# Where a decode kernel's late products, first gate and residual sum stand in its tail

## The chip, the core and the metric

The kernel runs on one core of a Trainium2 chip. Its engines are named as in the profile: PE is TensorE (matmuls; PEld are its weight loads), DVE is VectorE, ACT is ScalarE, POOL is GpSimd, and SP is SyncE, which here only issues transfers. The metric is the device time of one execution in microseconds. Everything is computed in fp32.

## The reference

One token of a transformer block at decode. The block has a modulation by a vector `c`, an attention over a cache of 8192 positions with 32 heads of 192, and a feed-forward part:

```python
mod = (_silu(c) @ w_mod).reshape(c.shape[0], 6, 1, -1)
sa, ca, ga, sb, cb, gb = (mod[:, 0], mod[:, 1], mod[:, 2], mod[:, 3], mod[:, 4], mod[:, 5])
h = _layernorm(x, axis=-1) * (1 + ca) + sa
x = x + ga * _A_ref(h, A_k_cache, A_v_cache, A_wq, A_wo)
h = _layernorm(x, axis=-1) * (1 + cb) + sb
x = x + gb * _B_ref(h, B_w1, B_b1, B_w2, B_b2)
```

`_A_ref` projects to queries with wq (640 x 6144), takes the softmax of the scores against the cached keys, sums the cached values, and projects back with wo (6144 x 640). `_B_ref` is w1 (640 x 1536), a squared ReLU, and w2 (1536 x 640). The six parts of `mod` have 640 numbers each; ga, sb, cb and gb are needed only after the attention.

## The kernel before

**The main loop.** The two caches of 32 heads are 201 MB each, and nearly all of the time goes into reading them once. A head's keys lie as 64 positions in each of 128 partitions. DVE multiplies them with the query and sums over the head's 192 (L282 to L291, `dve_keys`), POOL folds a small part, ACT takes the exponential (L306), and TensorE multiplies the probabilities with the values (L226, `pe_values`) in three column groups at once. Heads go in pairs, 16 of them. Keys lie in `k_t[0]` and `k_t[1]` by turns, values in `v_t[0]` and `v_t[1]`; SP refills a buffer when its last reader is done, all on one queue.

**After a pair.** `dve_project` (L318 to L333) takes the pair's sums of values out of PSUM: a reciprocal of the sums of the exponentials, then for each of the two heads a scaled and masked copy `om` (L327) and a sum `os` (L329). TensorE turns `os` into columns (`pe_turn`, `ps_oT`), DVE copies them to `oT`. `attend` (L308 to L316) is the output projection: DVE multiplies a pair's piece of wo with its three columns and adds to `acc`, three SCALAR_TENSOR_TENSOR of 128 x 640 (L315). For most pairs this happens in the loop, with the piece of wo behind the keys in `k_t[1]`.

**The tail.** The pieces of wo of pairs 11 to 14 come together in one transfer, `wot` in `v_t[0]`, and their products are the late ones: `attend_late`. `between` calls it for pairs 11, 12 and 13 (nine products), out of `dve_project` of the last pair, after the wait for the second head's values. Pair 14 follows after the copy of the last `oT`. The piece of the last pair is done by TensorE (L427) from `wm1` in `k_t[0]`, added in PSUM (`ps_att`) to the sum of `acc` over the partitions (L419).

The other tail transfers, in the order of SP's queue, are: `wot`; `wm1` (last piece of wo and the weights of ga, sb and cb); `w1g` in two pieces (w1, then the weights of gb) into `k_t[1]`; and w2 in four pieces (6, 3, 2 and 1 blocks of 12) into `v_t[1]`, which are issued when the last values are multiplied.

**Gates and the layernorm.** `mod(target, w, n, blocks)` (L154 to L160) multiplies silu(c) with the weights of n parts of 640, block by block of 32 rows, in four column groups of n x 160. In before, one call makes ga, sb and cb together (`ps_b`, 480 columns, five blocks). DVE copies them into `mods` and adds one to cb. The residual `x1` is `ps_att` times ga (L431) plus x (L432). `layernorm` (L167 to L183) sums x1 (L170), has TensorE total it over the partitions (L164), subtracts the mean, squares and sums (L176), totals again, and has ACT take the root (L178); a reciprocal (L181) and two DVE steps with cb and sb end it. Its argument `before` is a function called between the first total and DVE's wait for it, and `scale1` one called after ACT's root is issued; in before both do nothing in the tail.

**Feed-forward.** TensorE multiplies with w1 (L441), then makes gb (L159, 160 columns). DVE adds the bias, takes the maximum with zero, squares and transposes (L448 to L451); TensorE multiplies with w2 block by block (L466) and waits for each of the four pieces ahead of its blocks. DVE multiplies with gb and adds (L469, L470), and SP stores 640 numbers.

Each engine's instructions run in the order of the program text; a semaphore wait holds all that stands behind it on that engine.

Of the kernel before, what the change touches and what calls it, by code (L numbers as in the profile page):

```python
# [5 lines left out]
ALU = mybir.AluOpType  # L6
AX = mybir.AxisListType
# [3 lines left out]
D = 640  # L11
# [5 lines left out]
DG = D // G  # L17
FG = FF // G
KB = DG // 32
# [5 lines left out]
NPAIR = H // 2  # L25
# [4 lines left out]
WO = 3 * D  # L30
# [40 lines left out]
def block_kernel(nc, kw, ky, vc, wm0, wot, wm1, w1g, w2, out):  # L71
    sem = nc.alloc_semaphore
    V, A, L, T, S = (Line(nc, e, n) for e, n in ((nc.vector, "dve"), (nc.scalar, "act"), (nc.gpsimd, "pool"),
                                                 (nc.tensor, "pe"), (nc.sync, "sp")))
    v, act, pool, pe = nc.vector, nc.scalar, nc.gpsimd, nc.tensor
# [11 lines left out]
    def ps(name):  # L87
        return nc.alloc_psum_tensor(name, [P, 512], F32)
# [15 lines left out]
    ps_mx = [ps(f"ps_mx{s}") for s in range(2)]  # L104
    ps_sum, ps_oT, ps_q, ps_att = ps("ps_sum"), ps("ps_oT"), ps("ps_q"), ps("ps_att")
    ps_o = [ps(f"ps_o{s}") for s in range(2)]
# [47 lines left out]
    def mod(target, w, n, blocks):  # L154

        for b in blocks:
            wb = w[:, b * n * D:(b + 1) * n * D].rearrange("p (m n) -> p m n", m=n)
            for g in range(G):
                i = pe.matmul(target[32 * g:32 * (g + 1), :n * DG], e_t[:, b:b + 1].to_broadcast([P, 32]),  # L159
                              wb[:, :, DG * g:DG * (g + 1)], start=(b == 0), stop=(b == KB - 1))  # L160
        return T.mark(i)

    def total(col, src):
        i = pe.matmul(ps_sum[:, col:col + src.shape[1]], ones[:, :], src, start=True, stop=True)  # L164
        return T.mark(i)

    def layernorm(x, copies, s, m, xm, sq, ss, sd, rs, h, scale1, shift, col, ready, before):  # L167

        V.wait(ready)
        T.wait(V.mark(v.tensor_reduce(s, x, axis=AX.X, op=ALU.add)))  # L170
        m_t = total(col, s)
        before()
        V.wait(m_t)
        V.wait(V.mark(v.tensor_scalar(m, ps_sum[:, col:col + 1], 1.0 / (copies * D), None, op0=ALU.mult)))
        V.wait(V.mark(v.tensor_scalar(xm, x, m, None, op0=ALU.subtract)))
        T.wait(V.mark(v.scalar_tensor_tensor(sq, xm, 1.0, xm, op0=ALU.mult, op1=ALU.mult, accum_out=ss)))  # L176
        A.wait(total(col + 1, ss))
        m_sd = A.mark(act.activation(sd, ps_sum[:, col + 1:col + 2], AF.Sqrt, bias=eps_t[:, :], scale=1.0 / (copies * D)))  # L178
        sc1 = scale1()
        V.wait(m_sd)  # L180
        V.wait(V.mark(v.reciprocal(rs, sd)))  # L181
        V.wait(V.mark(v.scalar_tensor_tensor(h, xm, rs, sc1, op0=ALU.mult, op1=ALU.mult)))  # L182
        return V.mark(v.tensor_add(h, h, shift))  # L183
# [15 lines left out]
    s_, m_, ss_, sd_, rs_ = (piece(at + j, 1) for j in range(5))  # L199
    xm_, sq_ = piece(at + 5, KB), piece(at + 5 + KB, KB)  # L200
    m_h1 = layernorm(x_c, 1, s_, m_, xm_, sq_, ss_, sd_, rs_, h1[:, :], scale_a, maT[:, :KB, 0], 8, m_small, lambda: None)

    T.wait(m_h1)
    wq0 = v_t[1][:, KB * 2 * D:KB * 2 * D + WQ].rearrange("p (b n) -> p b n", b=KB)
    for b in range(KB):
        i = pe.matmul(ps_q[:, :PW], h1[:, b:b + 1].to_broadcast([P, P]), wq0[:, b], start=(b == 0), stop=(b == KB - 1))
# [4 lines left out]
    done = {}  # L211
# [97 lines left out]
    def attend(i, w, landed):  # L309

        w = w.rearrange("p (j n) -> p j n", j=NV)
        V.wait(landed)
        for j in range(NV):
            V.wait(V.last())
            V.mark(v.scalar_tensor_tensor(acc[:, :], w[:, j], oT[:, i, j:j + 1], acc[:, :], op0=ALU.mult, op1=ALU.add))  # L315
        done["wo", i] = V.last()  # L316

    def dve_project(i, between=lambda: None):  # L318

        V.wait(done["sum", i])  # L320
        V.wait(V.mark(v.reciprocal(r2[:, :], ps_sum[:, :2])))
        for a in range(2):
            n = 32 * NV
            V.wait(done["v", 2 * i + a])
            if a:
                between()
            V.wait(V.mark(v.scalar_tensor_tensor(om[:n], ps_o[a][:n].rearrange("p (d e) -> p d e", e=E), r2[:n, a:a + 1],  # L327
                                                 mask[:n, None, :].to_broadcast([n, ED, E]), op0=ALU.mult, op1=ALU.mult)))
            o = v.tensor_reduce(os_[:n, a], om[:n], axis=AX.X, op=ALU.add)  # L329
            if a == 0:  # L330
                V.wait(V.mark(o))
        o.then_inc(tk_o, 1)
# [5 lines left out]
    for h in range(H):  # L338
        s, i = h % 2, h // 2
        def between(c):  # L340
            if s == 0 and i and c == 0:
                dve_project(i - 1)
            if s and i and c == 0 and h in WITH_W:
                attend(i - 1, k_t[1][:, HD:], (k_sem[1][1], 16 * (i + 1)))

        dve_keys(h, between)
        if s == 0 and i:
            turned(i - 1)
        if s == 0 and i + 1 < NPAIR:
            evict_query(i + 1, done["q", i + 1])  # L350
        dve_max(h)
        if h + 1 < H:
            S.wait(*(m_wm0 if h == 0 else (done["v", h - 1],)))
            dma(v_t[1 - s][:, :], vc[h + 1], b_sem[1 - s])
        if h + 2 < H:
            S.wait(*done["k", h])
            if s == 0:
                S.wait(done["q", i + 1])
            elif h in WITH_W:
                S.wait(done["wo", i - 1])  # L360
            w = KSLOT if h + 2 in WITH_W else HD
            dma(k_t[s][:, :w], keys_of(h + 2), k_sem[s][1])


    wot_t, wm1_t, w1_t, w2_t = v_t[0], k_t[0], k_t[1], v_t[1]
# [9 lines left out]
    a = 0  # L375
    for n, b in enumerate(W2_CUT):
        dma(w2_t[:, a:b], w2[:, a:b], w_sem[3 + n])
        a = b
# [3 lines left out]
    def room(n):  # L382
        r = tail[0][:, :n]
        tail[0] = tail[0][:, n:]
        return r

    mods = room(4 * DG)
    x1, x_t, gb2, y, hT, cb1, xm2, sq2, h2 = (room(DG) for _ in range(9))
    f, fT = room(FG), room(FG)
    bbt, spr = room(32 * (FB + KB)), room(32 * (FB + KB))  # L390
    s2, m2, ss2, sd2, rs2 = (room(1) for _ in range(5))

    def spread(dst, src, n):
        s3 = spr[:, :32 * n]
        V.wait(V.mark(v.tensor_copy(s3.rearrange("p (b r) -> p b r", r=32), src[:, :, None].to_broadcast([P, n, 32]))))
        V.wait(V.mark(v.transpose(dst, s3)))

    def attend_late(i):
        at = (i - NPAIR + 1 + NTAIL) * WO
        attend(i, wot_t[:, at:at + WO], (w_sem[8], 16))  # L400
# [2 lines left out]
        for i in range(NPAIR - 1 - NTAIL, NPAIR - 2):  # L403
            attend_late(i)

    ps_b, ps_g, ps_f, ps_y = ps_mx[0], ps_mx[1], ps_o[0], ps_o[1]
    dve_project(NPAIR - 1, between)
    T.take(tk_o)
    m_turn = T.mark(pe.matmul(ps_oT[:, :NV], os_[:96].rearrange("p a d -> p (a d)"), quad[:96, :], start=True, stop=True))  # L409
    T.wait((w_sem[1], 16))  # L410
    m_b = mod(ps_b, wm1_t[:, WO:], 3, range(KB))
    V.wait(m_turn)
    m_oT = V.mark(v.tensor_copy(oT[:, NPAIR - 1], ps_oT[:, :NV]))
    attend_late(NPAIR - 2)
    V.wait(done["v", H - 2])
    spread(x_t, x_c, KB)
    T.wait(done["wo", NPAIR - 2])
    for g in range(G):
        pe.matmul(ps_att[32 * g:32 * (g + 1), :DG], ones[:, :32], acc[:, DG * g:DG * (g + 1)], start=True, stop=False)  # L419
    V.wait(m_b)  # L420
    v.tensor_copy(mods[:, :3 * DG], ps_b[:, :3 * DG])
    cb1_of = V.mark(v.tensor_scalar(cb1, ps_b[:, 2 * DG:3 * DG], 1.0, None, op0=ALU.add))
    wo = wm1_t[:, :WO].rearrange("p (j n) -> p j n", j=NV)
    T.wait(m_oT)
    for j in range(NV):
        for g in range(G):
            i = pe.matmul(ps_att[32 * g:32 * (g + 1), :DG], oT[:, NPAIR - 1, j:j + 1].to_broadcast([P, 32]),  # L427
                          wo[:, j, DG * g:DG * (g + 1)], start=False, stop=(j == NV - 1))
    m_att = T.mark(i)
    V.wait(m_att, cb1_of)  # L430
    V.wait(V.mark(v.tensor_mul(x1, ps_att[:, :DG], mods[:, :DG])))  # L431
    m_x1 = V.mark(v.tensor_add(x1, x1, x_t))  # L432
    m_h2 = layernorm(x1, 32, s2, m2, xm2, sq2, ss2, sd2, rs2, h2, lambda: cb1, mods[:, DG:2 * DG], 16, m_x1, lambda: None)
    V.wait(m_h2)
    m_hT = V.mark(v.transpose(hT, h2))  # L435
    T.wait(m_hT, (w_sem[2], 16))
    hT3 = hT.rearrange("p (b r) -> p b r", r=32)
    for b in range(KB):
        at = b * FF
        for g in range(G):  # L440
            i = pe.matmul(ps_f[32 * g:32 * (g + 1), :FG], hT3[:, b], w1_t[:, at + FG * g:at + FG * (g + 1)],  # L441
                          start=(b == 0), stop=(b == KB - 1))
# [16 lines left out]
    for b in range(FB):  # L459
# [4 lines left out]
        for g in range(G):  # L464
            o = b * D + DG * g
            i = pe.matmul(ps_y[32 * g:32 * (g + 1), :DG], fT3[:, b], w2_t[:, o:o + DG], start=(b == 0), stop=(b == FB - 1))  # L466
# [50 lines left out]
```

## Time and profile before

| | before |
|---|---|
| median of 3 runs | 1063.14 us (1063.02 to 1063.73) |
| the profiled execution, its own time | 1062.42 us |
| its span, first to last instruction | 1061.1 us |
| HBM read | 451.82 MB, 426 GB/s over the span |
| DVE busy | 867.6 us (82%) |
| PE busy | 441.3 us (42%) |
| POOL busy | 195.1 us (18%) |
| ACT busy | 32.9 us (3%) |
| mean granted clock of TensorE | 0.688 |

The profile is one execution. A busy share says how much of the span an engine worked, not whether the end waited for it. The timeline gives each instruction's start and length in us from the span's start; in brackets stands how long its engine was idle before it and what ended that. A fp32 matmul stands as two rows of the trace, so 20 matmuls count as x40. The chain that ended last is followed back from the last instruction. A transfer's time runs from its issue to its landing, and so includes its wait behind the earlier ones of the queue.

### The profile page before, as it was taken

To read this page: it belongs to the slowest core of one execution; us is meant where nothing else is said; L and a number is where in the kernel's file an instruction comes from. 1 tells how busy PE (TensorE), PEld (TensorE's weight loads), DVE (VectorE), ACT (ScalarE), POOL (GpSimd) and SP (SyncE) were. 2 spreads that over 40 slices of the span, in tenths; PEclk is the share of its full clock that TensorE was granted. 3 is DMA by queue.
4 is the path that set the end of the run, shared out by engine and by line. 5 is a ranking of instruction groups with operands and counts; after the bars stand their busy time and mean duration, and the time that the engine had idled before them with its cause. 6 is when DMAs were issued, how large, how long until landed. Compare 5 with 4: busy or idle time off the path is not lost. (4 is left out here: it accounts for less than half of the span.)

```text
span 1061.1 us, 5222 instructions
## 1 busy us (share of the span) xinstructions
PE 441.3 (42%) x2130; PEld 161.5 (15%) x2130; DVE 867.6 (82%) x445; ACT 32.9 (3%) x87; POOL 195.1 (18%) x71
## 2 busy tenths in 40 slices
PE   3135423254452336345243633425354434335337
PEld 1012111021120102112011211201111111112113
DVE  1885888988888988888898888899889797998964
ACT  1000000000000000000000000000000000000000
POOL 0221212212212221221221221222122122221210
PEclk9586657686665767666676665667666666767668
DMA  9999999999999999999999999999999999999994
GB/s 396 443 441 418 438 424 447 423 443 439 413 448 426 430 435 441 434 423 434 441 421 439 443 424 438 422 441 424 443 431 431 436 426 439 428 437 434 425 424 194
DMA packets 10675, 451.95 MB, mean 426 GB/s; under 512 B 1188, under 2 KB 1192, under 8 KB 1576
## 3 DMA queue, kind: packets, MB, share of 16 engines
q1 hardware_dynamic: 10664, 451.83, 98.7%
q8 instruction: 4, 0.07, 0.0%
q14 instruction: 7, 0.06, 0.0%
HBM read 451.82 MB, written 0.00 MB: 426 GB/s over the span
## 5 line engine op out<-in xcount | busy, mean ns | idle before, releaser
L282 DVE TENSOR_TENSOR k<-k,qb 128x6144 f32<-128x6144 f32 x64 | 419.4, 6553 | 112.5 <-DMA k<-in_kw 98.9
L285 POOL TENSOR_TENSOR k<-k 128x1344 f32<-128x1344 f32 x64 | 193.9, 3029 | 815.5 <-DVE k L282 815.5
L226 PE MATMUL ps_o<-v,p 128*32 128x512 f32 x1536 | 290.7, 732 | 20.0 <-PEq L60 20.0
L287 DVE TENSOR_REDUCE sc<-k 128x18 f32<-128x3456 f32 x64 | 240.2, 3753 | 2.2
L232 PE MATMUL ps_mx<-ident,mp 128*128 128x128 f32 x64 | 24.2, 480 | 456.6 <-PEq L60 456.6
L238 PE MATMUL ps_q<-k,h 128*128 128x384 f32 x160 | 86.7, 713 | 89.6 <-PEq L60 89.6
L226 PEld LDWEIGHTS ps_o<-v,p 128*32 128x32 f32 x1536 | 73.3, 131 | 213.2 <-issue 213.0
L291 DVE TENSOR_REDUCE sc<-k 128x14 f32<-128x1344 f32 x64 | 98.7, 1543 | 0.0
L232 PEld LDWEIGHTS ps_mx<-ident,mp 128*128 128x128 f32 x64 | 15.9, 308 | 471.7 <-issue 471.5
L238 PEld LDWEIGHTS ps_q<-k,h 128*128 128x128 f32 x160 | 44.1, 286 | 135.9 <-issue 131.2
L306 ACT ACTIVATE p<-sc,nm 128x256 f32<-128x256 f32 x32 | 16.2, 508 | 654.5 <-DVE nm L300 629.2
L300 DVE TENSOR_REDUCE nm<-ps_mx 128x1 f32<-128x128 f32 x32 | 9.3, 292 | 32.2 <-PE ps_mx L232 32.2
L315 DVE SCALAR_TENSOR_TENSOR acc<-k,oT,acc 128x640 f32<-128x640 f32 x33 | 29.2, 885 | 1.2
L327 DVE SCALAR_TENSOR_TENSOR om<-ps_o,r,mask 96x512 f32<-96x512 f32 x32 | 23.9, 747 | 1.1
L329 DVE TENSOR_REDUCE os<-om 96x64 f32<-96x512 f32 x32 | 21.8, 682 | 1.1
L215 ACT ACTIVATE qb<-ps_q 128x384 f32<-128x384 f32 x16 | 7.8, 490 | 311.1 <-PE ps_q L238 304.7
L315 DVE SCALAR_TENSOR_TENSOR acc<-v,oT,acc 128x640 f32<-128x640 f32 x12 | 10.6, 885 | 7.6 <-PE ps_o L226 7.2
L247 PE MATMUL ps_sum<-sp,ones 128*128 128x2 f32 x32 | 8.9, 349 | 18.7 <-PEq L60 18.7
L159 PE MATMUL ps_o<-v,silu 128*32 128x320 f32 x40 | 5.6, 741 | 14.4 <-DVE silu L152 14.4
L247 PEld LDWEIGHTS ps_sum<-sp,ones 128*128 128x128 f32 x32 | 8.0, 312 | 23.0 <-issue 23.0
L144 DVE COPY small<-v 128x27 f32<-128x27 f32 x1 | 0.2, 180 | 11.6 <-DMA v<-in_wm 11.6
L159 PE MATMUL ps_mx<-k,silu 128*32 128x480 f32 (+1 forms) x80 | 8.2, 568 | 0.0
(74 smaller groups left out, 80.4 us busy)
## 6 DMA issues: line engine op xcount, KB each, us to landing
v<-in_vc SPq DMA_DIRECT2D x32, 6144.0 KB, 39.0
k<-in_kw SPq DMA_DIRECT2D x25, 7104.0 KB, 36.1
k<-in_ky SPq DMA_DIRECT2D x6, 6144.0 KB, 35.7
k<-in_wm SPq DMA_DIRECT2D x1, 5760.0 KB, 28.5
v<-in_wm SPq DMA_DIRECT2D x1, 4173.5 KB, 12.6
k<-in_kw SPq DMA_DIRECT2D x1, 4032.0 KB, 28.5
v<-in_wot SPq DMA_DIRECT2D x1, 3840.0 KB, 15.3
k<-in_w1g SPq DMA_DIRECT2D x1, 3840.0 KB, 23.8
```

Source lines behind the costliest of these rows:

```text
L226: i = pe.matmul(ps_o[s][32 * g:32 * (g + 1), :], p_t[s][:, E * j:E * (j + 1)].rearrange("p e r -> p (e r)"), t[:, j, g], start=(j == 0), s ...
L232: return pe.matmul(ps_mx[s][:, :P], mp[s][:, :].to_broadcast([P, P]), ident[:, :], start=True, stop=True)
L238: i = pe.matmul(ps_q[:, :PW], h1[:, b:b + 1].to_broadcast([P, P]), w[:, b], start=(b == 0), stop=(b == KB - 1))
L247: return pe.matmul(ps_sum[:, :2], ones[:, :], sp[:, :], start=True, stop=True)
L282: m_mul = V.mark(v.tensor_mul(pr, pr, q[:, None, :].to_broadcast([P, HALF, DH])))
L285: m_fold = L.mark(pool.tensor_add(half, half, pr[:, KEEP:, DH // 2:]))
L287: o = v.tensor_reduce(r[:, :KEEP], pr[:, :KEEP], axis=AX.X, op=ALU.add)
L291: m_sc = V.mark(v.tensor_reduce(r[:, KEEP:], half, axis=AX.X, op=ALU.add))
L306: act.activation(p_t[s][:, :, :], sc[s][:, :, None].to_broadcast([P, NPOS, 32 // E]), AF.Exp, bias=nm[s][:, :], accum_out=sp[:, s:s + 1]). ...
L315: V.mark(v.scalar_tensor_tensor(acc[:, :], w[:, j], oT[:, i, j:j + 1], acc[:, :], op0=ALU.mult, op1=ALU.add))
L327: V.wait(V.mark(v.scalar_tensor_tensor(om[:n], ps_o[a][:n].rearrange("p (d e) -> p d e", e=E), r2[:n, a:a + 1], mask[:n, None, :].to_broad ...
L329: o = v.tensor_reduce(os_[:n, a], om[:n], axis=AX.X, op=ALU.add)
```

## The change

1. In `dve_project` the wait for a head's values moves behind the call of `between`. In the last pair, DVE's nine late products thus stand ahead of the wait for the last head's values. For the other pairs `between` is empty there.
2. `wm1` is laid out with ga's weights apart from those of sb and cb, with the same number of bytes. `mod` makes ga alone in five blocks (into `ps_a`, the bank `ps_q`), then two blocks of sb and cb (`ps_b`). Two further blocks come in `before`, between the two totals of the layernorm, and the last one in `scale_b`, behind the second total.
3. Pair 14's products stand ahead of DVE's wait for the last turn and the copy of `oT`. DVE copies ga alone ahead of the residual; sb's copy and cb plus one follow in `scale_b`, behind the second total and ahead of the reciprocal.
4. x1's addition becomes a SCALAR_TENSOR_TENSOR which also writes the sum to `s2`; `layernorm` with `summed=True` leaves out its own sum, and TensorE waits for x1.

```diff
-    def layernorm(x, copies, s, m, xm, sq, ss, sd, rs, h, scale1, shift, col, ready, before):
-
-        V.wait(ready)
-        T.wait(V.mark(v.tensor_reduce(s, x, axis=AX.X, op=ALU.add)))
+    def layernorm(x, copies, s, m, xm, sq, ss, sd, rs, h, scale1, shift, col, ready, before, summed=False):
+
+        if summed:
+            T.wait(ready)
+        else:
+            V.wait(ready)
+            T.wait(V.mark(v.tensor_reduce(s, x, axis=AX.X, op=ALU.add)))
         m_t = total(col, s)
         before()
...
         for a in range(2):
             n = 32 * NV
-            V.wait(done["v", 2 * i + a])
             if a:
                 between()
+            V.wait(done["v", 2 * i + a])
...
-    m_b = mod(ps_b, wm1_t[:, WO:], 3, range(KB))
+    w_a, w_b = wm1_t[:, WO:WO + KB * D], wm1_t[:, WO + KB * D:]
+    m_a = mod(ps_a, w_a, 1, range(KB))
+    mod(ps_b, w_b, 2, range(2))
+    attend_late(NPAIR - 2)
     V.wait(m_turn)
     m_oT = V.mark(v.tensor_copy(oT[:, NPAIR - 1], ps_oT[:, :NV]))
-    attend_late(NPAIR - 2)
     V.wait(done["v", H - 2])
     spread(x_t, x_c, KB)
+    V.wait(m_a)
+    V.mark(v.tensor_copy(mods[:, :DG], ps_a[:, :DG]))
...
-    V.wait(m_b)
-    v.tensor_copy(mods[:, :3 * DG], ps_b[:, :3 * DG])
-    cb1_of = V.mark(v.tensor_scalar(cb1, ps_b[:, 2 * DG:3 * DG], 1.0, None, op0=ALU.add))
...
-    m_x1 = V.mark(v.tensor_add(x1, x1, x_t))
-    m_h2 = layernorm(x1, 32, s2, m2, xm2, sq2, ss2, sd2, rs2, h2, lambda: cb1, mods[:, DG:2 * DG], 16, m_x1, lambda: None)
+    m_x1 = V.mark(v.scalar_tensor_tensor(x1, x1, 1.0, x_t, op0=ALU.mult, op1=ALU.add, accum_out=s2))
+    last = {}
+
+    def before():
+        mod(ps_b, w_b, 2, range(2, 4))
+
+    def scale_b():
+        last["b"] = mod(ps_b, w_b, 2, range(4, 5))
+        V.wait(last["b"])
+        V.mark(v.tensor_copy(mods[:, DG:2 * DG], ps_b[:, :DG]))
+        V.wait(V.mark(v.tensor_scalar(cb1, ps_b[:, DG:2 * DG], 1.0, None, op0=ALU.add)))
+        return cb1
+
+    m_h2 = layernorm(x1, 32, s2, m2, xm2, sq2, ss2, sd2, rs2, h2, scale_b, mods[:, DG:2 * DG], 16, m_x1, before, summed=True)
```

How the instructions stand on TensorE from the last turn on, first before the change (`ps_oT` is the turn, `ps_mx` with silu the gates, `ps_att` the projection, `ps_sum` the totals, `ps_o` the two feed-forward products):

```order
L409 MATMUL ps_oT<-quad,os 128x3
L159 MATMUL ps_mx<-k,silu 32x480 x20
L419 MATMUL ps_att<-acc,ones 32x160 x4
L427 MATMUL ps_att<-k,oT 32x160 x12
L164 MATMUL ps_sum<-v,ones 128x1 x2
L441 MATMUL ps_o<-k,v 32x384 x20
```

and now (`ps_q` with silu is ga, `ps_mx` with silu are sb and cb):

```order
L412 MATMUL ps_oT<-quad,os 128x3
L159 MATMUL ps_q<-k,silu 32x160 x20
L159 MATMUL ps_mx<-k,silu 32x320 x8
L426 MATMUL ps_att<-acc,ones 32x160 x4
L431 MATMUL ps_att<-k,oT 32x160 x12
L164 MATMUL ps_sum<-v,ones 128x1
L159 MATMUL ps_mx<-k,silu 32x320 x8
L164 MATMUL ps_sum<-v,ones 128x1
L159 MATMUL ps_mx<-k,silu 32x320 x4
L457 MATMUL ps_o<-k,v 32x384 x20
```

The gates of sb and cb are taken apart: two blocks stay ahead of the projection, two stand between the totals, and one behind them.

On DVE from the last pair's second head on, before the change (`om` and `os` are the copy and the sum of `dve_project`, `acc` the products, `v` the tail's small tiles in `v_t[0]`):

```order
L315 SCALAR_TENSOR_TENSOR acc<-v,oT,acc 128x640 x9
L327 SCALAR_TENSOR_TENSOR om<-ps_o,r,mask 96x512
L329 TENSOR_REDUCE os<-om 96x64
L413 COPY oT<-ps_oT 128x3
L315 SCALAR_TENSOR_TENSOR acc<-v,oT,acc 128x640 x3
L395 COPY v<-small 128x160
L396 STREAM_TRANSPOSE v<-v 128x160
L421 COPY v<-ps_mx 128x480
L422 TENSOR_SCALAR v<-ps_mx 128x160
L431 TENSOR_TENSOR v<-ps_att,v 128x160
L432 TENSOR_TENSOR v<-v 128x160
L170 TENSOR_REDUCE v<-v 128x1
```

and now:

```order
L318 SCALAR_TENSOR_TENSOR acc<-v,oT,acc 128x640 x9
L330 SCALAR_TENSOR_TENSOR om<-ps_o,r,mask 96x512
L332 TENSOR_REDUCE os<-om 96x64
L318 SCALAR_TENSOR_TENSOR acc<-v,oT,acc 128x640 x3
L419 COPY oT<-ps_oT 128x3
L398 COPY v<-small 128x160
L399 STREAM_TRANSPOSE v<-v 128x160
L423 COPY v<-ps_q 128x160
L435 TENSOR_TENSOR v<-ps_att,v 128x160
L436 SCALAR_TENSOR_TENSOR v<-v 128x160
```

The nine products stand in the same row as before: what moves is the wait for the last values, which held the first product and now holds `om` behind them. Pair 14's three products pass the copy of `oT`, and L170 is gone.

More of the change, by code (lines that the diff above doesn't have):

```diff
@@ L404, in between @@
             attend_late(i)
-    ps_b, ps_g, ps_f, ps_y = ps_mx[0], ps_mx[1], ps_o[0], ps_o[1]
+    ps_b, ps_g, ps_f, ps_y, ps_a = ps_mx[0], ps_mx[1], ps_o[0], ps_o[1], ps_q
     dve_project(NPAIR - 1, between)
@@ L429, in block_kernel @@
     m_att = T.mark(i)
-    V.wait(m_att, cb1_of)
+    V.wait(m_att, V.last())
     V.wait(V.mark(v.tensor_mul(x1, ps_att[:, :DG], mods[:, :DG])))
-    m_x1 = V.mark(v.tensor_add(x1, x1, x_t))
-    m_h2 = layernorm(x1, 32, s2, m2, xm2, sq2, ss2, sd2, rs2, h2, lambda: cb1, mods[:, DG:2 * DG], 16, m_x1, lambda: None)
+    m_x1 = V.mark(v.scalar_tensor_tensor(x1, x1, 1.0, x_t, op0=ALU.mult, op1=ALU.add, accum_out=s2))
[9 more added lines that the diff above has]
+    m_h2 = layernorm(x1, 32, s2, m2, xm2, sq2, ss2, sd2, rs2, h2, scale_b, mods[:, DG:2 * DG], 16, m_x1, before, summed=True)
     V.wait(m_h2)
@@ L506 @@
         "wot": w_late,
-        "wm1": np.concatenate([wo[-1], rows(wm[:, 2 * D:5 * D], KB)], axis=1),
+        "wm1": np.concatenate([wo[-1], rows(wm[:, 2 * D:3 * D], KB), rows(wm[:, 3 * D:5 * D], KB)], axis=1),
         "w1g": np.concatenate([rows(B_w1, KB), rows(wm[:, 5 * D:], KB)], axis=1),
```

## Prediction

> **What bounds the kernel now.** I read the page's queue line first, then the last 65 us in order of time, then the chain that ended last, then the landings of the last transfers.
>
> ```profile
> q1 hardware_dynamic: 10664, 451.83, 98.7%
> ```
>
> One queue keeps the 16 DMA engines at work for 98.7% of the span, so nothing ahead of the tail gets shorter unless fewer bytes are moved, and the change moves the same bytes. The tail is the exception: there the transfers end before the work does. The timeline of the tail (start, length, instruction, and in brackets what the engine waited for):
>
> ```profile
> 998.38 0.33 SPq L110 DMA_DIRECT2D v<-in_wot  x1
> 998.80 0.38 SPq L110 DMA_DIRECT2D k<-in_wm  x1
> ...
> 1013.53 0.80 SPq L110 DMA_DIRECT2D k<-in_w1g  x2
> ...
> 1016.32 8.89 PE L226 MATMUL ps_o<-v,p 128*32 128x512 f32 x48
> ...
> 1017.41 0.68 DVE L329 TENSOR_REDUCE os<-om 96x64 f32<-96x512 f32 x1
> ...
> 1025.33 8.25 DVE L315 SCALAR_TENSOR_TENSOR acc<-v,oT,acc 128x640 f32<-128x640 f32 x9 [7.23 <-PE ps_o L226]
> 1033.49 0.74 DVE L327 SCALAR_TENSOR_TENSOR om<-ps_o,r,mask 96x512 f32<-96x512 f32 x1
> ...
> 1035.59 6.65 PE L159 MATMUL ps_mx<-k,silu 128*32 128x480 f32 x40
> ...
> 1035.89 2.73 DVE L315 SCALAR_TENSOR_TENSOR acc<-v,oT,acc 128x640 f32<-128x640 f32 x3
> 1036.39 0.20 PEld L159 LDWEIGHTS ps_mx<-k,silu 128*32 128x32 f32 x4 [0.60 <-issue]
> ...
> 1038.88 0.34 DVE L396 STREAM_TRANSPOSE v<-v 128x160 f32<-128x160 f32 x1
> ...
> 1041.26 0.12 PEld L159 LDWEIGHTS ps_mx<-k,silu 128*32 128x32 f32 x4 [0.28 <-issue]
> ...
> 1042.96 0.32 DVE L422 TENSOR_SCALAR v<-ps_mx 128x160 f32<-128x160 f32 x1
> ```
>
> DVE stands idle for 7.23 us from 1018.09 (1017.41 + 0.68) until the last head's values are multiplied; then it does nine wo products (8.16 us, to 1033.49) which need none of those values, while TensorE stands idle. From TensorE's turn at 1035.10 on, the end hangs on this chain:
>
> ```profile
> 1035.10 0.56 PE ps_oT L409 x2
> ...
> 1042.24 0.27 PE ps_att L419 x8
> ...
> 1043.40 0.33 DVE v L431
> ...
> 1043.76 0.34 DVE v L432
> ...
> 1044.12 0.33 DVE v L170
> ...
> 1044.49 0.40 PE ps_sum L164 x2
> ...
> 1045.44 0.34 DVE v L176 x2
> ...
> 1045.83 0.40 PE ps_sum L164 x2
> ...
> 1046.55 0.17 DVE v L181
> ...
> 1047.92 4.86 PE ps_o L441 x40
> ...
> 1055.09 3.51 PE ps_o L466 x96
> ...
> 1058.63 0.34 DVE v L469
> ```
>
> Against it stand the landings. The transfers by tile (KB, then us from issue to landing), the times at which the four pieces of w2 are issued, and two stretches of a microsecond and two longer ones (PE, PEld, DVE, ACT, POOL busy, then TensorE's granted clock, the share of the DMA engines and GB/s):
>
> ```profile
> k<-in_wm SPq DMA_DIRECT2D x1, 5760.0 KB, 28.5
> v<-in_wot SPq DMA_DIRECT2D x1, 3840.0 KB, 15.3
> k<-in_w1g SPq DMA_DIRECT2D x1, 3840.0 KB, 23.8
> v<-in_w SPq DMA_DIRECT2D x1, 1920.0 KB, 20.6
> k<-in_w1g SPq DMA_DIRECT2D x1, 1600.0 KB, 27.3
> v<-in_w SPq DMA_DIRECT2D x1, 960.0 KB, 22.5
> v<-in_w SPq DMA_DIRECT2D x1, 640.0 KB, 23.5
> v<-in_w SPq DMA_DIRECT2D x1, 320.0 KB, 23.8
> ```
> ```profile
> L110 SPq DMA_DIRECT2D v<-in_w x4: 328/432/434, 1025.3 to 1026.6; - x4
> ```
> ```profile
> 1015.50:1025.30 9.80, 9.38 (x50) 2.61 (x50) 1.60 (x3) 1.47 (x3) 0.00 (x0) 0.77 1.00 433
> 1025.30:1035.10 9.80, 0.00 (x0) 0.03 (x1) 9.30 (x11) 0.00 (x0) 0.00 (x0) 0.75 0.95 405
> ```
> ```profile
> 1030.00:1031.00 1.00, 0.00 (x0) 0.00 (x0) 0.96 (x2) 0.00 (x0) 0.00 (x0) 0.64 1.00 430
> ...
> 1049.00:1050.00 1.00, 1.00 (x12) 0.35 (x8) 0.25 (x1) 0.00 (x0) 0.00 (x0) 0.50 0.05 20
> ```
>
> So wot is there at 1013.7 (998.38 + 15.3), wm1 at 1027.3, w1 at 1037.3, the last gate's weights at 1041.2 (issued about 1013.9). w2's pieces are issued in even steps from 1025.3 to 1026.6, hence land at 1045.9, 1048.2, 1049.6 and 1050.4. The engines are at work nearly without a pause up to there, so this is a floor. The second feed-forward product starts at 1055.09, 4.7 us after all of w2 is there: today the chain of work binds, with less than 8 us of room under it.
>
> **The change, part by part.** *The nine products.* They start at 1018.09, since wot landed 4.4 us before, and end at 1026.25, 1.0 us after the values' end (1025.21). Will they be slower beside matmuls? The three products at 1035.89 ran beside the gate's matmuls and took 2.73 us, 0.91 each, as the nine did alone (8.16 / 9 = 0.91). I charge nothing. From the evacuation at 1033.49 to the turn at 1035.10 is 1.61, so the turn stands at 1027.9 instead of 1035.10: 7.2 us gained. The gate behind it starts 0.49 later as before, at 1028.4, 1.1 after wm1's landing. That wait is next in line and just not reached.
>
> *The first gate alone.* In before a group of four loads takes 0.80 at half clock (0.20 + 0.60) and 0.40 at full (0.12 + 0.28), at 480 columns. By width, 160 columns take 0.27 or 0.13, and 320 take 0.53 or 0.27. Each block is two groups, since 20 matmuls stand as 40 in the trace. Gate a and two blocks of b are ten and four groups: 2.4 us at full clock, 4.8 at half (6.65 before). They end at 1030.8 or 1033.2. DVE in that time does pair 14's three products, which now stand ahead of the copy of oT (1027.75 + 2.73 = 1030.5); the copy, the spread and the gate's copy cost about 1.3 more (each by the 0.32 and 0.34 of L422 and L396), so DVE is free at 1031.8. TensorE's wo matmuls wait for that copy; they take 1.14 at full clock (1042.24 to 1043.40) or 2.2. The residual starts at 1032.0 or 1035.4, against 1043.40.
>
> *The sum with the addition.* L170 goes: 0.37 (1044.12 to 1044.49). The fused form costs 0.39 to TensorE's start (1045.44 to 1045.83) where the plain addition cost 0.36. Gain 0.34.
>
> *Gate b inside the layernorm.* From the residual to the first feed-forward product is 4.52 before (1043.40 to 1047.92). Blocks 2 and 3 stand on TensorE between the two totals: 1.07 at full clock, hidden beside DVE's 1.34 (1044.49 to 1045.83), but 2.13 at half, which delays the second total by about 0.95. Block 4, its copy and the addition of one (0.15 + 0.53 + 0.36 + 0.36, with 0.15 of start) reach the reciprocal 1.55 after the second total instead of 0.72: 0.83 lost, 1.36 at half clock. In all 5.0 or 6.5 us: the split costs 0.5 to 2.0 here, and never pays here.
>
> *Feed-forward.* At full clock its first product would stand at 1037.0, and waits for w1 until 1037.4; at half clock at 1041.9. From there to the second product is 7.17 before (a matmul stretch that is part half, part full clock, then four DVE steps): 5.5 if all full (ten groups of 0.32, and 2.3), 8.7 if all half. So the second is ready at 1042.9, or 1049.1 with half clock up to 1041.9 and before's mixture after it.
>
> *The floor.* Twelve blocks of w2 take 3.51, 0.29 each. Ready at 1042.9, TensorE does six from 1045.9, three from 1048.2, two from 1049.6 and the last from 1050.4: the final product of DVE starts at 1050.8 instead of 1058.63. That is 7.8 us earlier; the chain alone would give 12.1 (1042.9 + 3.5 = 1046.4, and the final product at 1046.5), and 4.3 of it is lost to the landings. Ready at 1049.1 the matmuls end at 1052.6: 6.0 us earlier, with nothing lost to them. At half clock throughout the feed-forward pieces after a 1045.9 start, at most twice 3.51, they end at 1052.9. What follows (two DVE steps and the store, 2.4 us) is untouched.
>
> The profiled execution takes 1062.42 (span 1061.1), the median is 1063.14, 0.72 above it. Subtracting 7.8: span 1053.3, own time 1054.6, median 1055.3.
>
> *The clock.* Which column of these sums holds depends on TensorE's pause, now 2.7 us (1025.2 to 1027.9). In before the clock stayed full until 1030.4 (0.64 in the row of 1030), five us into a pause. That row favours full clock here. The Trainium skill (TensorE: Matmul & The Clock Gate, What's actually happening) says that it halves after at least one idle window of about 3.4 us, and rises after about one busy window. By that rule the pause is too short, and the sum would be the full column's, held by the floor. The row agrees as far as it goes; that a pause of 2.7 us always keeps the clock, no row here shows.
>
> **The rivals.** *TensorE's chain ends last.* If the clock is half from the turn to the first feed-forward product, the final step is at 1052.6 and the time 1057.1. Half throughout would give 1050.6 + 7.0 = 1057.6 and 1062.1, but in before the clock rose within 6 us of steady matmuls (0.20 + 0.60 at 1036.39, 0.12 + 0.28 at 1041.26), and here they are steady for 4 to 7 us. Chance 0.14.
>
> *The floor is lower.* In the row of 1049 the DMA share is 0.05, about one engine of 16: the others are done some 2 to 3 us earlier. If that engine does not lag in other executions, w2 is there near 1047.7, the matmuls end near 1048.1, and the time is 1052.6. The Trainium skill (DMA: Bandwidth & Descriptors, Latency and other measured facts) lists two of the engines as usually slower than the rest, with a cause that it calls a guess. By that the lag is regular and the floor holds; one execution can't tell. Chance 0.06.
>
> *It does not do what it says.* Were wot later than the values' end, DVE would wait there and the products stay where they were. Then only the small terms remain, from -1.9 (4.8 for 6.65 at the gate) to +1.2 (2.0 lost in the layernorm, 0.8 won ahead of it at half clock): 1061.3 to 1064.3. It must be over 11.5 us later than in this trace. Chance 0.04.
>
> *Slower: the products beside the values slow the transfers.* The stretch with the products moves 405 GB/s, the one before it 433, so such an effect is not excluded. The floor lies 35 us after 1015.5; to end 2.1 us later than before it would have to be 10 us further off, a rate lower by 22% over all of it. At 25% lower it is 11.7 us later and the time 1067. Against it: the rows differ by 6%, and the products are only moved, not added. Chance 0.02.
>
> **How the numbers follow.** The forecast, the floor of w2 at 1055.3, has 0.74; its own range is 1054.5 to 1056.2 (the executions of before lie 0.7 apart). The range that should hold 8 in 10 takes in most of the half-clock case: 1054.2 to 1057.6. A measurement of this kernel can tell about 0.2%, 2.1 us, from no change. The first three cases (0.74, 0.14, 0.06) are all faster by more: 0.94; the fourth is within it, 0.04; slower 0.02.
>
> **What would show it.** After: DVE's nine products start near 1018.1, at 0.91 each; the turn is near 1027.9; the first feed-forward product starts at 1037.4 to 1042, waiting for w1 if at the lower end; the second product's matmuls stand in pieces with gaps before the landings, the last pair of groups right behind the landing near 1050.4; DVE's final product near 1050.8. I am wrong if the second product runs as one block of 3.5 us that starts after 1047.5 (the chain binds), if w2 lands at another time than 1050.4 by more than 1 us, or if the products start after 1025.

## The result, and the profile after

| | before | changed |
|---|---|---|
| median, us | 1063.31 (4 runs, 1063.02 to 1063.73) | 1054.92 (4 runs, 1054.80 to 1055.10) |
| ratio, 95% interval | | 0.9921 [0.9904, 0.9938] |
| the profiled execution, own time | 1062.42 | 1055.00 |
| its span | 1061.1 | 1053.6 |

The changed kernel is 8.4 us faster; 7.8 had been forecast. First, the tail in order of time: DVE's products, the turn, the gates, and the two feed-forward products.

```profile
1018.27 8.25 DVE L318 SCALAR_TENSOR_TENSOR acc<-v,oT,acc 128x640 f32<-128x640 f32 x9
1025.87 1.75 SPq L110 DMA_DIRECT2D v<-in_w  x4
1026.44 0.74 DVE L330 SCALAR_TENSOR_TENSOR om<-ps_o,r,mask 96x512 f32<-96x512 f32 x1
...
1028.04 0.56 PE L412 MATMUL ps_oT<-quad,os 96*128 96x3 f32 x2 [2.23 <-PEq L60]
1028.53 2.90 PE L159 MATMUL ps_q<-k,silu 128*32 128x160 f32 x40
...
1031.20 1.33 PE L159 MATMUL ps_mx<-k,silu 128*32 128x320 f32 x16
...
1033.69 0.32 DVE L435 TENSOR_TENSOR v<-ps_att,v 128x160 f32<-128x160 f32 x1 [1.80 <-PE ps_att L431]
...
1039.05 3.43 PE L457 MATMUL ps_o<-k,v 128*32 128x384 f32 x40 [2.03 <-DVE v L451]
...
1044.20 0.58 DVE L467 STREAM_TRANSPOSE v<-v 128x384 f32<-128x384 f32 x1
...
1046.09 1.84 PE L482 MATMUL ps_o<-v 128*32 128x160 f32 x48 [2.24 <-DMA v<-in_w]
1048.30 1.02 PE L482 MATMUL ps_o<-v 128*32 128x160 f32 x24 [0.38 <-DMA v<-in_w]
1049.81 1.25 PE L482 MATMUL ps_o<-v 128*32 128x160 f32 x24 [0.49 <-DMA v<-in_w]
1051.13 0.33 DVE L485 TENSOR_TENSOR v<-ps_o,v 128x160 f32<-128x160 f32 x1 [5.42 <-PE ps_o L482]
```

Look at the brackets of L482. The second product's input is ready at 1044.8 (1044.20 + 0.58); the product starts at 1046.09, released by a transfer, and waits twice more for one. Before, it was one block of 3.5 us released by DVE. The chain that ended last says the same:

```profile
1026.72 23.05 DMA v<-in_w
1049.77 0.04 issue
1049.81 0.75 PE ps_o L482 x16
1050.56 0.02 issue
1050.58 0.52 PE ps_o L482 x8
1051.10 0.02 issue
1051.13 0.34 DVE v L485
```

In before it led back through TensorE and DVE to the turn; now it leads to w2's third piece, and from there to its issue. The end has passed from the work to the transfers.

### The profile page after: what moved, and what is told of

Same layout as the page of the kernel before. It is cut to its first block, busy times and chain, and to the rows that moved or that the text cites. A ratio compares the mean times of both kernels' runs of the same rounds, so it can differ in the third digit from the quotient of the medians.

```text
span 1053.6 us, 5304 instructions
## 1 busy us (share of the span) xinstructions
PE 444.6 (42%) x2170; PEld 164.3 (16%) x2170; DVE 867.1 (82%) x446; ACT 32.9 (3%) x87; POOL 195.3 (19%) x71
## 5 line engine op out<-in xcount | busy, mean ns | idle before, releaser
L241 PE MATMUL ps_q<-k,h 128*128 128x384 f32 x160 | 89.2, 731 | 88.1 <-PEq L60 88.1
L330 DVE SCALAR_TENSOR_TENSOR om<-ps_o,r,mask 96x512 f32<-96x512 f32 x32 | 23.9, 747 | 1.1
L298 DVE TENSOR_REDUCE mp<-sc 128x1 f32<-128x64 f32 x32 | 7.0, 220 | 1.1
```

## The experiments

Two theories were tried. *Landing theory*: the changed kernel ends when w2's last pieces are there, and what the chain over TensorE and DVE would give beyond that is lost. *Chain theory*: that chain still ends last, so each part counts in full. Each ratio is to runs of before on the same chip.

**w2 taken away.** The second product multiplies with the late pieces of wo instead of w2, which isn't loaded.

```diff
-    S.wait(done["v", H - 1])
-    a = 0
-    for n, b in enumerate(W2_CUT):
-        dma(w2_t[:, a:b], w2[:, a:b], w_sem[3 + n])
-        a = b
...
-        for n, c in enumerate(W2_CUT):
-            if b * D < c:
-                T.wait((w_sem[3 + n], 16))
-                break
+        T.wait((w_sem[8], 16))
...
-            i = pe.matmul(ps_y[32 * g:32 * (g + 1), :DG], fT3[:, b], w2_t[:, o:o + DG], start=(b == 0), stop=(b == FB - 1))
+            i = pe.matmul(ps_y[32 * g:32 * (g + 1), :DG], fT3[:, b], wot_t[:, o:o + DG], start=(b == 0), stop=(b == FB - 1))
```

In the changed kernel:

> The changed kernel without the four transfers of w2: the second feed-forward product multiplies with the late pieces of wo, which lie in the same number of columns; so w2's load is left out and the output is another. Landing theory: the second product starts when its input is there, near 1044.85 instead of 1046.09, runs as one block of 3.5 us, and the final step of DVE is at 1048.4 instead of 1051.13: 2.7 us faster, 1052.2. Chain theory: unchanged, 1054.9.

Measured: 1052.28 (1052.14 to 1054.14, 4 runs), ratio 0.9902 [0.9887, 0.9917]. In before:

> Before without the four transfers of w2 (its second feed-forward product multiplies with the late pieces of wo; w2's load is left out and the output is another). Both theories: in before nothing waits for w2, so no change, 1063.3. If it gets faster by more than 0.5 us, the transfers cost something else than their landing (the traffic beside the tail's work), and the gain of the changed kernel without w2 is not the landing's alone.

Measured: 1064.03 (1062.23 to 1064.33, 11 runs), ratio 1.0005 [0.9996, 1.0014]. The intervals of the changed kernel with and without w2 overlap. Three of its four executions without w2 take 1052.14 to 1052.40, as the landing theory has it; the fourth takes 1054.14, which neither theory says and no trace shows. The trace of the one at 1052.14 decides for the profiled executions, here its first and second feed-forward products:

```profile
1039.04 3.43 PE L452 MATMUL ps_o<-k,v 128*32 128x384 f32 x40 [2.04 <-DVE v L446]
...
1044.82 3.47 PE L474 MATMUL ps_o<-v 128*32 128x160 f32 x96 [0.99 <-DVE v L462]
```

Up to the first product it is the same as with w2 (1039.04 against 1039.05). Then the second starts at 1044.82, released by DVE, as one block. DVE's final step is at 1048.36 against 1051.13: the landings cost the changed kernel 2.8 us in that execution, and before nothing.

**More bytes ahead of w2.** One more transfer in the queue, 1.38 MB that nothing reads:

```diff
-    w_sem = [sem(f"w{n}") for n in range(10)]
+    w_sem = [sem(f"w{n}") for n in range(11)]
...
     dma(w1_t[:, KB * FF:W1G], w1g[:, KB * FF:], w_sem[9])
+    dma(wm1_t[:, W1M:KSLOT], w1g[:, :KSLOT - W1M], w_sem[10])
...
-    S.wait(m_out)
+    S.wait(m_out, (w_sem[10], 16))
```

> The changed kernel with one more transfer in the queue ahead of w2: 2688 columns of w1 once more (1.38 MB, 1344 KB), into columns that nothing reads. At 430 GB/s it takes 3.2 us. Landing theory: every piece of w2 lands 3.2 us later and the time goes up by as much: 1058.1. Chain theory: the extra bytes go into the room under the chain, 1054.9 to 1055.4.

> Before, with the same extra transfer of 1.38 MB ahead of w2. w2's last piece would land near 1053.6 instead of 1050.4, and the second feed-forward product starts at 1055.09. Both theories: nothing waits for it, no change: 1063.3. If the time goes up by 3.2 us here too, the extra transfer costs time in some other way than through w2's landing, and the run above says nothing.

Measured: changed 1058.97 (1058.41 to 1059.18, 5 runs), ratio 0.9959 [0.9946, 0.9973]; before 1063.55 (1061.61 to 1064.41, 11 runs), ratio 0.9998 [0.9989, 1.0007]. The same bytes cost before nothing and the changed kernel about 4 us. That is 0.9 more than forecast. The chain of the changed kernel with the extra bytes, in its fastest execution (1058.41):

```profile
1026.61 22.68 DMA v<-in_w
1049.29 0.14 issue
1049.42 5.18 PE ps_o L483 x96
1054.60 0.02 issue
1054.62 0.34 DVE v L486
```

The first piece lands at 1049.29, 3.3 later. Then TensorE needs 5.18 us for the 96 matmuls instead of 3.5, without a wait: after the longer pause ahead of them its clock is half for part of them (0.67 in the mean of that stretch). In this execution that adds little: the final step is 3.5 later than in the changed kernel's trace (1054.62 against 1051.13), the landing 3.3. Where the rest of the 0.9 by the medians comes from is not shown.

**The parts apart.** Part 1 alone is before with the one wait moved; it was run with w2 and without. Parts 2 to 4 alone are the changed kernel with that wait put back.

```diff
-            V.wait(done["v", 2 * i + a])
             if a:
                 between()
+            V.wait(done["v", 2 * i + a])
```

> Part 1 alone: before, with the nine products ahead of the wait for the last values; gates, layernorm and residual as before. Landing theory (the changed kernel's end is set by the last landing of w2, and only the moved products are needed to reach it): the turn near 1028.0, all three gates in 5 to 6 us behind it, the second feed-forward product ready near 1045.7, ahead of the first piece of w2 or just behind it, so the time is that of the changed kernel within 0.4 us: 1054.8 to 1055.3. Chain theory (the chain over TensorE and DVE still ends last, so every part adds up): later by what the other parts give, about 1 us: 1055.8 to 1056.5.

Measured: 1055.38 (1054.88 to 1055.70, 5 runs), ratio 0.9924 [0.9910, 0.9938], by which it is not told from the changed kernel; the median lies just beyond the landing theory's range and short of the chain theory's. But its trace is not what the landing theory said:

```profile
1028.38 5.83 PE L159 MATMUL ps_mx<-k,silu 128*32 128x480 f32 x40
...
1039.90 6.09 PE L441 MATMUL ps_o<-k,v 128*32 128x384 f32 x40 [1.71 <-DVE v L435]
...
1048.35 3.47 PE L466 MATMUL ps_o<-v 128*32 128x160 f32 x96 [1.00 <-DVE v L451]
```

The second product is ready at 1048.35, not 1045.7, and runs as one block that DVE releases: here the chain ends last, by a little. Most of the difference is the first product: 6.09 us for the 3.43 of the changed kernel's trace, since the clock is half for most of it (0.54 in the mean from 1039.9 to 1045.8).

> Part 1 alone, without the transfers of w2 in the same way. With no landing of w2 in the way, parts 2 to 4 should show what they are worth behind the moved products. Landing theory: slower than the changed kernel without w2 by about 1 us: 1053.0 to 1053.5, and faster than part 1 alone with w2 by 1.5 to 2. Chain theory: the same difference of about 1 us, but no gain against part 1 alone with w2.

Measured: 1054.69 (1054.23 to 1055.91, 5 runs), ratio 0.9920 [0.9907, 0.9934]. That is 0.7 below part 1 with w2, with intervals that overlap, and not the 1.5 to 2 of the landing theory: for part 1 alone w2 hardly binds. Against the changed kernel without w2 it is 2.4 us more, not 1. Two stretches of it, the layernorm and the first product (PE, PEld, DVE, ACT, POOL busy, then clock, DMA share, GB/s):

```profile
1036.00:1039.40 3.40, 0.77 (x4) 0.59 (x4) 1.98 (x9) 0.26 (x1) 0.00 (x0) 1.00 0.47 197
1040.20:1044.80 4.60, 4.59 (x40) 1.57 (x44) 1.30 (x2) 0.00 (x0) 0.00 (x0) 0.69 0.02 6
```

and the changed kernel without w2:

```profile
1036.00:1039.40 3.40, 1.36 (x20) 0.57 (x21) 2.19 (x7) 0.26 (x1) 0.00 (x0) 1.00 0.41 173
1039.00:1042.30 3.30, 3.26 (x43) 1.34 (x46) 1.33 (x2) 0.00 (x0) 0.00 (x0) 1.00 0.05 17
```

The first product starts 1.2 us earlier with the split gates (1039.04 against 1040.21) and takes 3.43 instead of 4.80 us, at a clock of 1.00 instead of 0.69. The matmuls of gates sb and cb between the totals not only hide there; they keep TensorE busier (1.36 us of the 3.4 against 0.77) ahead of the product. When that holds the clock, and when not, is taken up in the last section. In all traces of this study the first product takes 4.8 to 6.1 us in the five without split gates, and 3.43 us in six of the nine with them (5.1 in the other three).

> Parts 2 to 4 alone: the gates split, pair 14's products earlier, the sum with the addition, but DVE's nine products behind the last values as before. Both theories: no landing binds here, so the parts show their own worth. From the turn to the residual 5.65 us in the changed kernel against 8.30, from there to the first feed-forward product 5.36 against 4.52: 1.8 us faster, 1061.5. At half clock behind the longer pause up to 1 us less of it: 1061.3 to 1062.5. If the gates inside the layernorm cost the 2 us that half clock would cost there, no gain: 1063.3 or more.

Measured: 1062.37 (1060.40 to 1063.30, 11 runs), ratio 0.9990 [0.9981, 0.9999]: 1.1 us faster by the medians, inside the range for half clock, with an interval that all but reaches 1. So parts 2 to 4 together are a gain, if a small one, where no landing binds; the split was not run alone.

**A longer chain.** Three or six more products on DVE behind the nine, into spare columns:

```diff
+    spare = room(D)
...
             attend_late(i)
+        V.wait(V.last())
+        for _ in range(3):
+            V.wait(V.mark(v.scalar_tensor_tensor(spare, wot_t[:, :D], oT[:, 0, :1], acc[:, :], op0=ALU.mult, op1=ALU.add)))
```

> The changed kernel with three more products of 128 x 640 on DVE behind the nine, into columns that nothing reads: 2.7 us more on the chain ahead of the last head's evacuation. Landing theory: the second feed-forward product is ready near 1047.5 instead of 1044.8, its blocks catch up behind w2's pieces, and the end moves by 0 to 0.3 us: 1054.9 to 1055.2. Chain theory: 2.7 us slower, 1057.6.

Measured: 1055.15, 1055.11, 1057.26, 1057.49 and 1057.91, ratio 0.9933 [0.9920, 0.9947].

> The same with six more products, 5.4 us more on the chain. Landing theory: the second feed-forward product is ready near 1050.2, when all of w2 is there, and runs 3.5 us as one block: final step near 1053.8, 2.7 us slower, 1057.6; so the first three cost nothing and the next three their full price. Chain theory: 5.4 us slower, 1060.3.

Measured: 1060.05 (1057.67 to 1060.13, 6 runs), ratio 0.9964 [0.9952, 0.9976]. Neither theory holds all executions: two of delay3's and two of delay6's six (1057.67, 1057.77) are where the landing theory put them, the others where the chain theory did. The trace of a late execution of delay3 tells why the trial was a poor one:

```profile
1030.81 0.56 PE L417 MATMUL ps_oT<-quad,os 96*128 96x3 f32 x2 [5.78 <-PEq L60]
1031.29 2.90 PE L159 MATMUL ps_q<-k,silu 128*32 128x160 f32 x40
...
1043.11 5.13 PE L462 MATMUL ps_o<-k,v 128*32 128x384 f32 x40 [2.03 <-DVE v L456]
...
1050.59 3.47 PE L487 MATMUL ps_o<-v 128*32 128x160 f32 x96 [0.99 <-DVE v L472]
```

The extra products also lengthen TensorE's pause ahead of the turn (5.78 us), and the first product ran 1.7 us longer, with a mean clock of 0.67. Ready at 1050.6, the second has used up the room. The pause alone does not decide that clock: in delay6's trace, of its fastest execution, the pause is 8.55 us and the first product takes 3.43. So the delay was put in once more behind the first product, where it changes no pause ahead of the gates:

```diff
-    V.wait(V.mark(v.tensor_scalar(f, f, 0.0, None, op0=ALU.max)))
+    for _ in range(7):
+        V.wait(V.mark(v.tensor_scalar(f, f, 0.0, None, op0=ALU.max)))
```

> The changed kernel with the maximum with zero between the two feed-forward products done seven times instead of once (0.39 us each, the same output): 2.35 us more on the chain, in a place that leaves TensorE's pauses ahead of the gates, and so its clock there, as they are. Landing theory: the second product is ready near 1047.2 instead of 1044.8, catches up behind w2's pieces, and the end stays: 1054.8 to 1055.3. Chain theory: 2.4 us slower, 1057.3.

Measured: 1055.02, 1055.27, 1056.41, 1056.67 and 1058.23, ratio 0.9938 [0.9925, 0.9952]. The profiled execution (1055.27):

```profile
1041.88 2.73 DVE L466 TENSOR_SCALAR v<-v 128x384 f32<-128x384 f32 x7
...
1045.24 0.58 DVE L468 STREAM_TRANSPOSE v<-v 128x384 f32<-128x384 f32 x1
...
1046.18 5.22 PE L483 MATMUL ps_o<-v 128*32 128x160 f32 x96 [3.13 <-DMA v<-in_w]
```

Ready at 1045.8 (1045.24 + 0.58) even so, since the first gate ran at full clock there, the transfer still releases the product: 2.35 us of extra work cost 0.3. In a second execution they cost 0.1, in the other three 1.5 to 3.3 against the changed kernel's median, so that the median of all five lies between the two theories. The changed kernel's own trace has 2.8 us of room (1051.1 less 3.5 is 1047.6, against ready at 1044.8), which 2.35 and a first product at 5.1 instead of 3.4 overrun by 1.3. That is near the two in the middle, though no trace shows it; the last stays open. The landing theory holds for the changed kernel as it is, by a room of 2.8 us in its trace, which a first product at 5.1 would make 1.1, and no longer for one with more work in its tail.

**TensorE's pause filled.** The changed kernel without w2, with eight matmuls that nothing needs between the values and the turn:

```diff
     dve_project(NPAIR - 1, between)
+    T.wait((w_sem[8], 16))
+    for b in range(2):
+        for g in range(G):
+            pe.matmul(ps_g[32 * g:32 * (g + 1), :480], e_t[:, b:b + 1].to_broadcast([P, 32]),
+                      wot_t[:, 480 * g:480 * (g + 1)], start=True, stop=True)
     T.take(tk_o)
```

> The changed kernel without the transfers of w2, and with eight matmuls of 480 columns on TensorE between the last values and the turn, on landed data and into a bank that is overwritten later: they fill 1.6 of the 2.2 us of TensorE's pause. Clock theory (the granted clock falls to a half in the first gate because of that pause): it stays full, gates and projection take 1.2 to 1.6 us less, 1050.6 to 1051.0 against 1052.2 without the filling. If the clock falls all the same, or if the gate is held by wm1's landing (28.36 after the thousand) anyway: 1052.0 to 1052.4.

Measured: 1052.33 (1051.10 to 1052.58, 4 runs), ratio 0.9899 [0.9884, 0.9914]. By the median it gains nothing. In the profiled execution, the fastest, the first gate takes 1.56 us instead of 2.89, and the second product starts at 1043.66 instead of 1044.82:

```profile
1028.67 1.56 PE L159 MATMUL ps_q<-k,silu 128*32 128x160 f32 x40
...
1043.66 3.47 PE L479 MATMUL ps_o<-v 128*32 128x160 f32 x96 [0.52 <-DVE v L467]
```

That is near the clock theory's 1050.6 to 1051.0; the median lies in the other range. The other three executions are a microsecond or more later and have no trace, so whether filling the pause helps in general is inconclusive.

**w2's last pieces dealt otherwise.** Each of the last three in two transfers, 120 and 8 partitions:

```diff
-        dma(w2_t[:, a:b], w2[:, a:b], w_sem[3 + n])
+        if n == 0:
+            dma(w2_t[:, a:b], w2[:, a:b], w_sem[3 + n])
+        else:
+            dma(w2_t[:120, a:b], w2[:120, a:b], w_sem[3 + n])
+            dma(w2_t[120:, a:b], w2[120:, a:b], w_sem[3 + n])
...
-                T.wait((w_sem[3 + n], 16))
+                T.wait((w_sem[3 + n], 16 if n == 0 else 32))
```

> The changed kernel with each of the last three pieces of w2 issued as two transfers, partitions 0 to 119 and 120 to 127, so that the bytes may be dealt to the DMA engines in another way; bytes and order are the same. Lagging-engine theory (the last 2 us of the landings are one engine's backlog, and the dealing moves work off it): w2 is all there near 1048.6, the last matmuls end near 1049.0, the final step of DVE is 1.5 to 2 us earlier: 1053.0 to 1053.5. If the dealing does not move work off that engine, or all engines end together anyway: 1054.9 to 1055.3, or later if 120 partitions go over fewer engines.

Measured: 1059.71 (1059.33 to 1060.14, 6 runs), ratio 0.9967 [0.9955, 0.9980]: 4.8 us worse than the changed kernel. Two stretches of it:

```profile
1043.00:1047.00 4.00, 1.19 (x36) 0.87 (x28) 2.88 (x7) 0.00 (x0) 0.00 (x0) 1.00 0.93 237
1047.00:1050.00 3.00, 0.23 (x4) 0.23 (x8) 0.00 (x0) 0.00 (x0) 0.00 (x0) 0.67 0.87 207
```

The DMA engines are as busy as in the changed kernel (0.93 against 0.89 from 1043 to 1047), but move 237 GB/s there against its 363. The first piece, issued as before, lands at 1049.64 (23.9 us after its issue, against 20.1). Whether one lagging engine makes the last 2 us of the landings was thus not answered: the dealing itself was slower. That the time follows the later landing is one more mark of the landing theory.

## Why the prediction was right

*The products.* They started at 1018.27 (forecast 1018.09) and took 8.25 us beside the values' matmuls, as much as alone. The turn came at 1028.04 (1027.9). The wait for wm1, called just not reached, was nearer than that: wm1 landed at 1028.4 (issued at 999.41, 29.0 us), not 1027.3, 0.1 ahead of the first gate.

*The clock.* Here a step failed. The pause of TensorE, 2.2 us, was held to be too short, by the row of before and by the Trainium skill (TensorE: Matmul & The Clock Gate, What's actually happening), which wants an idle window of about 3.4 us. The first gate took 2.90 us instead of the 1.33 put for full clock, which itself was too little: at full clock it takes 1.56, as with the pause filled above. Stretches of the changed kernel, the pause and the first gate:

```profile
1025.80:1028.00 2.20, 0.01 (x3) 0.00 (x0) 2.17 (x4) 0.00 (x0) 0.00 (x0) 0.99 1.05 454
1028.50:1031.20 2.70, 2.70 (x41) 2.00 (x45) 2.60 (x6) 0.00 (x0) 0.00 (x0) 0.50 0.95 410
```

and of the kernel with seven maxima, whose pause is longer:

```profile
1025.40:1028.10 2.70, 0.00 (x0) 0.00 (x0) 2.63 (x5) 0.00 (x0) 0.00 (x0) 1.00 1.04 450
1028.50:1029.90 1.40, 1.38 (x41) 1.33 (x44) 1.33 (x3) 0.00 (x0) 0.00 (x0) 1.00 0.92 395
```

A pause of 2.2 us halved the clock in the one, one of 2.7 us left it full in the other. So it is not the pause's length alone that decides.

*The chain.* The residual started at 1033.69 (forecast 1032.0 at full clock, 1035.4 at half), the first product 5.36 us behind it (5.0 to 6.5), the second's input was ready at 1044.8 (1042.9 to 1049.1). All lie between the two columns, with the clock half in the first gate and full from there. That the 5.36 is above the full column's 5.0 is a matter of sizes: gate b's blocks 2 and 3 took 1.28 us instead of 1.07, so the second total stood 1.52 behind the first instead of 1.34, and the reciprocal 1.72 behind that instead of 1.55. Two small misreadings changed nothing: the row of 1030 puts the fall of the clock in before at 1030.3, not 1030.4, and TensorE's wo matmuls took 1.16 there, not 1.14.

*The floor.* w2's pieces released the second product near 1046.1, 1048.3 and 1049.8, as forecast (1045.9, 1048.2, 1049.6). This term set the end, and the 1.9 us by which the chain was later than forecast vanished under it. The last piece took 0.52 us of matmuls, not 0.29, at full clock (1.00 in the microsecond of 1050): the final step stands at 1051.13, not 1050.8.

*The sum.* The span was forecast at 1053.3 and is 1053.6. The 0.72 added for the median over the profiled execution was wrong: the changed kernel's median lies 0.08 below its profiled execution. Between the two profiled executions the gain is 7.4 us (7.8 forecast); the 8.4 of the medians is 1.0 more because before's profiled execution lies 0.9 below its median, the changed kernel's 0.1 above. In 56 further runs before lies between 1061.94 and 1064.50, a spread of 2.6 us; the changed kernel's four runs lie within 0.3. With the chain ending last what varies in it, the clock above all, can show in the time; under the landings it does not. The two errors, 0.4 too early for the profiled execution (1054.6 against 1055.00) and 0.8 too late for the median, partly cancel, by luck, and leave 1055.3 against 1054.92.

*The rivals.* TensorE's chain did not end last in the changed kernel, but it nearly does: part 1 alone and the longer chains show it there. A lower floor was not seen: in the seven traces that load w2 as it is and nothing more, its last piece lands between 1050.4 and 1050.7. The lag that the doubt was about stands in all seven, with a DMA share of 0.07 to 0.15 from 1048 to 1049 and 0.05 to 0.13 from 1049 to 1050. So the engines are not "at work nearly without a pause" up to the last landing, as the prediction says in one place; most of them are done earlier, as it says in this rival. The slower rival is out: the nine products ran at an unchanged 0.91 each, and w2's first piece was there 20.1 us after its issue (20.6 before).

## What to carry to other kernels

Work that an in-order engine could do while it waits belongs ahead of the wait: one moved line gave nearly all of the 8 us, and the splits and fusions around it gave about 1 us alone and none that the time shows on top. Before summing up what a shorter chain gives, look up when the last transfer lands: it is the floor, and what the chain gains below it only becomes room. That room is still worth something, since it takes in variations of the clock.

## What the runs showed of the hardware

The clock changes at steps of a fixed grid. In before the mean of 0.64 in the microsecond of 1030 puts the fall at 1030.3; the rise (0.74 in that of 1040) is at 1040.5, the next fall (0.67 in that of 1047) at 1047.3: 10.2 and 6.8 us apart, three and two times 3.4. Here are the microseconds of the changed kernel around its change:

```profile
1027.00:1028.00 1.00, 0.00 (x0) 0.00 (x0) 0.97 (x3) 0.00 (x0) 0.00 (x0) 0.97 1.07 461
...
1031.00:1032.00 1.00, 1.00 (x20) 0.57 (x16) 0.53 (x2) 0.00 (x0) 0.00 (x0) 0.82 1.06 446
```

They put its fall at 1027.9 and its rise at 1031.4, 3.4 apart. The Trainium skill (TensorE: Matmul & The Clock Gate, What's actually happening) has a free-running window of 3413 ns, with which this agrees. What differs is its idle window: a step of the grid that was mostly, not wholly, idle was enough here. The grid lies otherwise in each trace, so the traces can be compared step by step, with the steps counted in 3.41 us from each trace's own changes of the clock. Here are (columns as above) one step each of the changed kernel, of the kernel with seven maxima, and of that with w2 dealt otherwise:

```profile
1024.52:1027.94 3.42, 1.29 (x11) 0.12 (x3) 3.31 (x6) 0.00 (x0) 0.00 (x0) 1.00 0.97 418
1033.78:1037.19 3.41, 1.86 (x26) 0.60 (x17) 1.91 (x8) 0.26 (x1) 0.00 (x0) 1.00 0.98 414
1034.37:1037.78 3.41, 1.31 (x18) 0.55 (x18) 1.96 (x7) 0.26 (x1) 0.00 (x0) 1.00 1.02 432
```

TensorE is busy for 1.29, 1.86 and 1.31 us of them. Behind the first and the third the clock halves, behind the second it stays full. The first holds most of the changed kernel's pause. In the two others the first feed-forward product starts at almost the same time, 1037.73 and 1037.71, and takes 3.43 and 5.12 us.

The same holds for that product in all fourteen traces. In the five without split gates the last step ahead of it is busy for 0.22 to 0.29 of its length, and the product begins at half clock. In three of the nine with split gates a step that ends 0.1 to 0.4 us into the product is busy for 0.38 to 0.40, and it takes 5.1 us. In the other six no step that ends just ahead of the product or within it is below 0.49, and it takes 3.43 us. By this the gates between the totals hold the clock where enough of them falls into one step. For the pause ahead of the first gate the share is not the whole rule: the clock stays full behind steps of 0.45 (w2 dealt otherwise) and 0.54 (seven maxima), but halves behind 0.51 in the changed kernel with more bytes and in part 1 without w2.

Transfers of 120 and 8 partitions in place of 128 took the rate down to 207 to 237 GB/s with the DMA engines 87 to 93% busy, in the one trace there is of them.
